# Issuing every DMA of a spectral mixer's forward and backward pass on SyncE's queue

## The chip, the cores and the metric

The kernel runs on one core of a Trainium2 chip. Its time is the device time of one execution in microseconds; several runs are made and the median is given. The five engines of the core are named as in the profile: PE (TensorE), DVE (VectorE), ACT (ScalarE), POOL (GpSimd) and SP (SyncE). A DMA is issued by an engine and carried out by the core's 16 DMA engines. In this kernel SP and ACT issue through a hardware queue each (q1 and q10 in the profile), POOL through a software queue (q0). DMA transposes are issued on SP alone.

## The reference

One pre-LayerNorm block with two mixers, x of 2048 x 448 in bfloat16, and all its gradients:

```python
def _A_ref(x, w_r, w_i):                      # spectral mixer
    X = rfft2(x.astype(float32), axes=(-2, -1))        # 2048 x 225 complex
    return irfft2(X * (w_r + 1j * w_i), s=(S, D)).astype(bfloat16)

def _B_ref(x, w1, b1, w2, b2):                # token MLP, F = 1792
    u = gelu(einsum("bsd,sf->bdf", layernorm(x), w1) + b1)
    return (einsum("bdf,fs->bds", u, w2) + b2).transpose(0, 2, 1)

h  = x + _A_ref(layernorm(x), w_r, w_i)
h2 = h + _B_ref(layernorm(h), w1, b1, w2, b2)
# outputs: h2, then the gradients of x, w_r, w_i, w1, b1, w2, b2 for grad_out
```

## The kernel before

The Fourier transforms are matrix products with tables of sines that the kernel makes itself: POOL writes counters (iota) and masks, DVE reduces the arguments, ACT takes the sines. A row transform (d_stage) is followed by a two-step column transform (s1_stage, s2_stage), and the inverse by s2_inv and inv_rows. Between the steps the rows are regrouped by small SP copies through SBUF: D2 (r_72 in the profile, written at L459) and D3 (r_73, written at L506).

In order of time, with the names that the prediction uses:

1. **Front.** x (xn, four loads on ACT, L193) and grad_out (go_tp, four loads on POOL, L194) come in. `load_w2T` (L187) brings rows of w2 in transposed on SP, into three buffers. The gradient of the hidden layer, dg = w2T x go (L567), is the filler: a generator that `fill(n)` advances by n matmuls between the steps of the spectral part. `fold_prep` (L433 to L437) folds pairs of LayerNorm rows into one of three buffers rF on DVE, and SP transposes them into rT. The spectral weights w_r and w_i are loaded by `w_io` (L398 and L400), 18 DMAs of 16 partitions each in rows of 225 elements, on POOL, into rG.
2. **Forward spectral stage.** s2_stage multiplies by the weights; the spectrum is kept in HBM (xspec_d, L615).
3. **Hidden layer (U stage).** `load_w1c` (L624) brings 256 columns of w1 at a time, two buffers, on POOL. The result of gelu and its derivative are made on ACT and DVE.
4. **Y stage.** `load_w2c` (L666) does the same for w2, into two buffers; L732 multiplies, `y_tail` (L737 to L740) loads the row of h from h_d on SP, adds on DVE and stores out_0 on POOL. Meanwhile SP transposes grad_out into goT (L719, L721) and the bias gradient (L714), which POOL stores (L715).
5. **dh stage.** SP transposes w1 (L789), L809 multiplies, `ln_bwd` (L777 to L783) is the LayerNorm backward, and the row transform of the spectral backward begins.
6. **Backward spectral stage.** SP transposes du (L818); POOL clears the pad columns (L819) and loads w_r and w_i again with `w_io`, into rD. Filler now are the gradients of w2 (L865, `gw2_gen`) and of w1 (L880, `gw1_gen`): `stream` (L851) transposes their left operands on SP into three buffers rst, the results go through ACT or DVE (L868, L883) into three buffers rO, and POOL stores them (L870, L885). The gradients of w_r and w_i are stored by `w_io` on POOL (L398).
7. **Tail.** For every one of 16 row blocks inv_rows ends in `gx_consumer`: an x load on SP (L901), ln_bwd, and the store of the gradient of x on SP (L905). Its buffers come from a ring of eight, five per step, so that DVE's tmp of a step (L781) takes the buffer from which the step before stores.

PE's order is written out by hand. The order on the other engines, SP's queue included, comes from a scheduler that goes by program order and its own estimate of when each instruction is ready. An instruction waits in its queue until its semaphores are there, and the next one behind it waits too.

Of the kernel before, what the change touches and what calls it, by code (L numbers as in the profile page):

```python
# [16 lines left out]
P = 128  # L17
S = 2048
D = 448
DF = 225  # L20
KW = 226
F = 1792
NFB = 14
# [36 lines left out]
def kernel(  # L60
# [138 lines left out]
    gp_.dma_start(out=gtail[:, 0:DC], in_=grad_out[0][S - 16:S, 3 * DC:D])  # L199

# [421 lines left out]
    def load_w1c(jp):  # L622
        w = w1c_ring.next()
        gp_.dma_start(out=w, in_=B_w1.rearrange("(p t) f -> p t f", t=NT)[:, :, 256 * jp:256 * jp + 256])  # L624
        return w
# [29 lines left out]
    gp_.dma_start(out=smr[0:NFB, 0, :], in_=B_b1.rearrange("(j p) -> j p", p=P))  # L655
    gp_.dma_start(out=smr[:, 1, :], in_=B_b2.rearrange("(j p) -> j p", p=P))
    for i, dst in ((0, b1col), (1, b2col)):
# [6 lines left out]
    def load_w2c(i):  # L664
        w2cs[i] = w2c_ring.next()
        gp_.dma_start(out=w2cs[i], in_=B_w2.rearrange("(j p) s -> p j s", p=P)[:, :, 256 * i:256 * i + 256])  # L666

# [46 lines left out]
    nc.sync.dma_start_transpose(out=gb1r[:], in_=gb1b[:])  # L714
    gp_.dma_start(out=out_5.rearrange("(j p) -> j p", p=P), in_=gb1r[0:NFB, :])  # L715

# [37 lines left out]
    for t in range(3, NT):  # L754
        py = ps_mm()
        y_head(t, 0, NFB, py)
        y_tail(t, py)
        gb2_part(t)
        if t == NT - 1:
            for q in range(3):  # L760
                gb2_part(q)
            ve.tensor_copy(out=gb2b[:], in_=gb2[:])
            gp_.dma_start(out=out_7.rearrange("(p t) -> p t", t=NT), in_=gb2b[:])
        if t % 2 == 1 and t // 2 + 2 < NT // 2:
            load_w2c(t // 2 + 2)
# [53 lines left out]
    gp_.memset(W_view_B[:, :, :, DF:KW], 0.0)  # L819
    w_io(W_view_B, A_w_r, A_w_i, False, gp_)  # L820
    srow = mem.tile([P, KW], BF16, name="srow")
# [37 lines left out]
    def gw2_gen():  # L859
        for j, gt in stream(NFB, rE):  # L860
            o = ost.next()
            for c in range(4):
                pw = ps_mm()
                for k in range(4):
                    nc.tensor.matmul(pw[:], lhsT=gt[0:DC, k, :], rhs=goT[0:DC, k, c * 512:(c + 1) * 512],  # L865
                                     start=(k == 0), stop=(k == 3))
                    if k == 3:
                        evac(out=o[:, c * 512:(c + 1) * 512], in_=pw[:])  # L868
                        if c == 3:
                            gp_.dma_start(out=out_6[j * P:(j + 1) * P, :], in_=o)  # L870
                    yield

    def gw1_gen():
        for t, ht in stream(NT, rB):
            o = ost.next()
            for c in range(4):
                n = 4 if c < 3 else 2
                pw = ps_mm()
                for k in range(4):
                    nc.tensor.matmul(pw[:, 0:n * P], lhsT=ht[0:DC, k, :], rhs=du_t[0:DC, 4 * c:4 * c + n, k, :],  # L880
                                     start=(k == 0), stop=(k == 3))
                    if k == 3:
                        evac(out=o[:, c * 512:c * 512 + n * P], in_=pw[:, 0:n * P])  # L883
                        if c == 3:
                            gp_.dma_start(out=o4[:, t, :], in_=o[:, 0:F])  # L885
                    yield
# [9 lines left out]
    s2_stage(bwd_mult, N_FILL_B[3], N_FILL_B[4])  # L896
    w_io(W_view_B, out_2, out_3, True, gp_)

# [40 lines left out]
```

## Time and profile before

| | |
|---|---|
| median of 3 runs | 554.54 us (553.81 to 555.45) |
| the profiled execution, its own time | 558.94 us |
| its span, first to last instruction | 556.8 us |
| mean granted PE clock | 0.876 |
| busy: PE, DVE, ACT, POOL | 386.8, 259.5, 232.8, 119.1 us |
| DMA bytes by queue: q1 (SP), q0 (POOL), q10 (ACT) | 43.41, 42.26, 1.84 MB |

The profile is one execution. Its slices are fortieths of the span, each digit a busy share in tenths. A line of the timeline has start and duration in us, the engine, the line of the kernel, the operation with output and input, and in brackets how long the engine had been idle and what ended that. "SPq" is SP's queue of issues; neighbouring instructions of one line are merged into one row, with their count and the time from the first start to the last end. In a line of the DMA queues stand packets, MB and the share of the time of 16 engines that the packets took; these shares add up to more than 1 where packets of two queues overlap. In the view by stretches each line has the stretch, its length, busy time and number of instructions of PE, PE's weight loads, DVE, ACT and POOL, then the granted clock, the DMA share (the sum of the queues) and GB/s.

### The profile page before, as it was taken

What the parts mean: (1) busy time and instruction counts of PE and PEld (TensorE: products, weight loads), DVE (VectorE), ACT (ScalarE), POOL (GpSimd) and SP (SyncE); (2) the same over time, 40 slices, a digit from 0 to 9 for tenths busy, and PEclk for the clock granted to TensorE, in tenths of its full rate; (3) what the DMA queues carried; (4) which work ended last, traced back from release to release, by engine and by line L of the source; (5) the groups of instructions that cost most, each with busy time, mean ns of one, the idle gap of its engine ahead of it and who ended that gap; (6) DMA issues with size and microseconds to landing.
All of it is one profiled execution on the core that took longest, in us unless ns stands there. A gap on an engine that the chain in (4) does not pass through costs nothing.

```text
span 556.8 us, 6068 instructions
## 1 busy us (share of the span) xinstructions
PE 386.8 (69%) x1920; PEld 192.2 (35%) x1920; DVE 259.5 (47%) x710; ACT 232.8 (42%) x477; POOL 119.1 (21%) x177
## 2 busy tenths in 40 slices
PE   0135287485739888986779999935449998399990
PEld 0012154141325444442334455512114443145540
DVE  6643176364207857770122877500005674035655
ACT  2131076173416554420122244723206877158882
POOL 8232059700100011030331000023111102411110
PEclk9967599796879999997798999977758999879995
DMA  9999979759956665259963999799995798986552
GB/s 121 216 97 111 131 137 171 118 141 178 214 131 144 221 202 161 77 129 142 233 187 115 175 191 201 149 217 77 69 102 198 188 208 165 141 224 193 182 175 83
DMA packets 137344, 87.89 MB, mean 158 GB/s; under 512 B 111136, under 2 KB 127584, under 8 KB 137184
## 3 DMA queue, kind: packets, MB, share of 16 engines
q1 hardware_dynamic: 125248, 43.41, 48.2%
q0 software_dynamic: 11488, 42.26, 33.4%
q10 hardware_dynamic: 576, 1.84, 1.4%
q8 instruction: 15, 0.25, 0.2%
q14 instruction: 17, 0.14, 0.1%
HBM read 29.40 MB, written 23.89 MB: 96 GB/s over the span
## 4 chain that ended last, share of the span: by engine, by line
DMA 41%; PE 21%; issue 14%; DVE 10%; POOL 7%; ACT 4%; SPq 2%; DVEq 0%; POOLq 0%; ACTq 0%
PE ps_mm L809 6%; PE ps_mm L732 5%; DMA rS<-in_B_w_dram 5%; DMA out_dram<-r_81 4%; DMA rG<-in_A_w_r_dram 4%; DMA r_72<-in_B_w_dram 4%; DMA rD<-in_A_w_i_dram 4%; DMA r_73<-r_78 3%; DMA rE<-in_B_w_dram 3%; DMA rC<-rD 3%; PE ps_mm L880 3%; PE ps_mm L865 2%; DMA xspec_d<-rS 2%; DMA rD<-in_A_w_r_dram 2%; DMA out_dram<-rO 2%
## 5 line engine op out<-in xcount | busy, mean ns | idle before, releaser
L567 PE MATMUL ps_mm<-rC,rE 128*128 128x448 bf16 x224 | 62.9, 418 | 50.0 <-DMA rE<-in_B_w_dram 50.0
L865 PE MATMUL ps_mm<-rG,rst 112*128 112x512 bf16 x224 | 59.7, 418 | 23.4 <-DMA rst<-rE 12.9
L732 PE MATMUL ps_mm<-rE,rS 128*128 128x448 bf16 x224 | 51.0, 396 | 15.5 <-DMA rS<-in_B_w_dram 15.5
L880 PE MATMUL ps_mm<-rC,rst 112*128 112x512 bf16 (+1 forms) x256 | 54.9, 363 | 3.3 <-ACT rO L883 2.0
L567 PEld LDWEIGHTS <-rE 128*128 128x128 bf16 x224 | 24.5, 113 | 78.5 <-DMA rE<-in_B_w_dram 51.6
L687 PE MATMUL ps_mm<-rB,r_72 128*128 128x448 bf16 x224 | 43.5, 353 | 6.6 <-DMA r_72<-in_B_w_dram 4.4
L809 PE MATMUL ps_mm<-rD,r_73 128*128 128x448 bf16 x224 | 43.5, 353 | 0.6 <-DMA r_73<-in_B_w_dram 0.6
L868 ACT CAST rO<-ps_mm 128x512 bf16<-128x512 f32 x54 | 30.4, 598 | 29.7 <-DMA out_dram<-rO 20.5
L865 PEld LDWEIGHTS <-rst 112*128 112x128 bf16 x224 | 23.6, 106 | 55.0 <-issue 20.9
L732 PEld LDWEIGHTS <-rS 128*128 128x128 bf16 x224 | 23.8, 108 | 42.5 <-DMA rS<-in_B_w_dram 17.2
L880 PEld LDWEIGHTS <-rst 112*128 112x128 bf16 x256 | 24.8, 100 | 26.2 <-issue 4.1
L883 ACT CAST rO<-ps_mm 128x512 bf16<-128x512 f32 (+1 forms) x61 | 30.4, 562 | 3.7 <-PE ps_mm L880 1.8
L528 PE MATMUL ps_ff<-csI,rAT 113*128 113x448 bf16 x128 | 31.2, 369 | 0.8 <-ACT rAT L517 0.5
L687 PEld LDWEIGHTS <-r_72 128*128 128x128 bf16 x224 | 21.6, 98 | 28.3 <-DMA r_72<-in_B_w_dram 5.9
L517 ACT CAST rAT<-ps_ff 113x512 bf16<-113x512 f32 x32 | 18.6, 589 | 30.2 <-PE ps_ff L514 30.2
L739 DVE SCALAR_TENSOR_TENSOR r_81<-ps_mm,b2col,r_81 128x448 bf16<-128x448 f32 x16 | 10.6, 681 | 43.9 <-DMA r_81<-h_d 37.3
L744 ACT ACTIVATE r_81<-rC 128x448 bf16<-128x448 bf16 x16 | 9.2, 576 | 51.9 <-DVE r_81 L739 38.9
L450 ACT CAST r_78<-ps_ff 128x452 bf16<-128x452 f32 x32 | 17.1, 539 | 30.7 <-PE ps_ff L447 30.5
L870 POOL DMA_DIRECT2D out_dram<-rO x14 | 7.5, 537 | 103.2 <-ACT rO L868 91.0
L809 PEld LDWEIGHTS <-r_73 128*128 128x128 bf16 x224 | 21.7, 97 | 22.9 <-issue 1.8
L514 PE MATMUL ps_ff<-RTm,r_73 128*113 128x128 bf16 x128 | 13.4, 235 | 18.5 <-DMA r_73<-r_78 18.2
L463 DVE TENSOR_SCALAR r_72<-r_72 128x904 bf16<-128x904 bf16 x8 | 2.7, 391 | 48.5 <-DMA r_72<-r_78 48.5
(211 smaller groups left out, 684.7 us busy)
## 6 DMA issues: line engine op xcount, KB each, us to landing
r_72<-in_B_w_dram POOLq DMA_DIRECT2D x7, 1024.0 KB, 7.1
rS<-in_B_w_dram POOLq DMA_DIRECT2D x8, 896.0 KB, 7.7
out_dram<-rO POOLq DMA_DIRECT2D x14, 512.0 KB, 5.6
out_dram<-rO POOLq DMA_DIRECT2D x16, 448.0 KB, 3.1
r_72<-r_78 SPq DMA_DIRECT2D x32, 113.0 KB
r_73<-r_78 SPq DMA_DIRECT2D x32, 113.0 KB
xspec_d<-rS SPq DMA_DIRECT2D x8, 226.0 KB
rS<-xspec_d SPq DMA_DIRECT2D x8, 226.0 KB
```

Source lines behind the costliest of these rows:

```text
L450: sc.copy(out=ab, in_=pv)
L514: nc.tensor.matmul(pa[0:KC, i * P:(i + 1) * P], lhsT=D3[:, s1, c_, KC * ch:KC * ch + KC], rhs=RTm[:], start=True, stop=True)
L517: sc.copy(out=aT[0:KC].rearrange("p a b -> p (a b)"), in_=pa[0:KC, :])
L528: nc.tensor.matmul(py[:, 0:D], lhsT=aT[0:KC, i, :], rhs=csI[0:KC, i // 2, i % 2, :], start=(i == 0), stop=(i == 3))
L567: nc.tensor.matmul(pg[:, 0:D], lhsT=wT[:, t, :], rhs=go_tp[:, t, :], start=(t == 0), stop=(t == NT - 1))
L687: nc.tensor.matmul(pu[:, 0:D], lhsT=w1c[:, t, jj * P:(jj + 1) * P], rhs=hln[:, t, :, :], start=(t == 0), stop=(t == NT - 1))
L732: nc.tensor.matmul(py[:, 0:D], lhsT=w2cs[t // 2][:, j, (t % 2) * P:(t % 2 + 1) * P], rhs=g_[:, j, :, :], start=(j == 0), stop=(j == NFB - 1))
L809: nc.tensor.matmul(pdh[:, 0:D], lhsT=wT[:, j, :], rhs=du[:, j, :, :], start=(j == 0), stop=(j == NFB - 1))
L865: nc.tensor.matmul(pw[:], lhsT=gt[0:DC, k, :], rhs=goT[0:DC, k, c * 512:(c + 1) * 512], start=(k == 0), stop=(k == 3))
L868: evac(out=o[:, c * 512:(c + 1) * 512], in_=pw[:])
L880: nc.tensor.matmul(pw[:, 0:n * P], lhsT=ht[0:DC, k, :], rhs=du_t[0:DC, 4 * c:4 * c + n, k, :], start=(k == 0), stop=(k == 3))
L883: evac(out=o[:, c * 512:c * 512 + n * P], in_=pw[:, 0:n * P])
```

## The change

Every DMA that ACT or POOL issued is issued by SP instead, on its hardware queue, in program order with the transposes: the loads of x and grad_out, the spectral weights' loads and stores, the biases, the chunks of w1 and w2, h_d's store, and the stores of out_0 and of the gradients of w1, w2 and the biases. POOL keeps its memsets, iotas and masks. Nothing else is changed; sizes, buffers and program order stay.

```diff
     for q in range(4):
-        nc.scalar.dma_start(out=xn[:, 4 * q:4 * q + 4, :], in_=x_pt[:, 4 * q:4 * q + 4, :])
-        gp_.dma_start(out=go_tp[:, 4 * q:4 * q + 4, :], in_=go_tp_d[:, 4 * q:4 * q + 4, :])
+        nc.sync.dma_start(out=xn[:, 4 * q:4 * q + 4, :], in_=x_pt[:, 4 * q:4 * q + 4, :])
+        nc.sync.dma_start(out=go_tp[:, 4 * q:4 * q + 4, :], in_=go_tp_d[:, 4 * q:4 * q + 4, :])
         if q < 2:
             w2Ts.append(load_w2T(q))
...
-    w_io(W_view_F, A_w_r, A_w_i, False, gp_)
+    w_io(W_view_F, A_w_r, A_w_i, False, nc.sync)
...
     def load_w1c(jp):
         w = w1c_ring.next()
-        gp_.dma_start(out=w, in_=...)
+        nc.sync.dma_start(out=w, in_=...)
...
-    gp_.dma_start(out=h_d.rearrange("(p t) d -> p t d", t=NT), in_=hn)
+    nc.sync.dma_start(out=h_d.rearrange("(p t) d -> p t d", t=NT), in_=hn)
...
     def load_w2c(i):
         w2cs[i] = w2c_ring.next()
-        gp_.dma_start(out=w2cs[i], in_=...)
+        nc.sync.dma_start(out=w2cs[i], in_=...)
...
     for q in range(2):
-        gp_.dma_start(out=go_pt[:, 8 * q:8 * q + 8, :], in_=go_pt_d[:, 8 * q:8 * q + 8, :])
+        nc.sync.dma_start(out=go_pt[:, 8 * q:8 * q + 8, :], in_=go_pt_d[:, 8 * q:8 * q + 8, :])
...
-        gp_.dma_start(out=out_0[0, t * P:(t + 1) * P, :], in_=h2)
+        nc.sync.dma_start(out=out_0[0, t * P:(t + 1) * P, :], in_=h2)
...
-    w_io(W_view_B, A_w_r, A_w_i, False, gp_)
+    w_io(W_view_B, A_w_r, A_w_i, False, nc.sync)
...
-                            gp_.dma_start(out=out_6[j * P:(j + 1) * P, :], in_=o)
+                            nc.sync.dma_start(out=out_6[j * P:(j + 1) * P, :], in_=o)
...
-                            gp_.dma_start(out=o4[:, t, :], in_=o[:, 0:F])
+                            nc.sync.dma_start(out=o4[:, t, :], in_=o[:, 0:F])
...
-    w_io(W_view_B, out_2, out_3, True, gp_)
+    w_io(W_view_B, out_2, out_3, True, nc.sync)
```

The same is done to the 16-row tail of grad_out (gtail), to the two bias loads, and to the stores of out_5 and out_7.

More of the change, by code (lines that the diff above doesn't have):

```diff
@@ L198 @@
     gp_.memset(gtail[:], 0.0)
-    gp_.dma_start(out=gtail[:, 0:DC], in_=grad_out[0][S - 16:S, 3 * DC:D])
+    nc.sync.dma_start(out=gtail[:, 0:DC], in_=grad_out[0][S - 16:S, 3 * DC:D])
     s448, s128, s2048 = _sin_scale(448), _sin_scale(128), _sin_scale(2048)
@@ L623, in load_w1c @@
         w = w1c_ring.next()
[L624 removed]
+        nc.sync.dma_start(out=w, in_=B_w1.rearrange("(p t) f -> p t f", t=NT)[:, :, 256 * jp:256 * jp + 256])
         return w
@@ L714 @@
     nc.sync.dma_start_transpose(out=gb1r[:], in_=gb1b[:])
-    gp_.dma_start(out=out_5.rearrange("(j p) -> j p", p=P), in_=gb1r[0:NFB, :])
+    nc.sync.dma_start(out=out_5.rearrange("(j p) -> j p", p=P), in_=gb1r[0:NFB, :])
     for c in range(3):
@@ L762 @@
             ve.tensor_copy(out=gb2b[:], in_=gb2[:])
-            gp_.dma_start(out=out_7.rearrange("(p t) -> p t", t=NT), in_=gb2b[:])
+            nc.sync.dma_start(out=out_7.rearrange("(p t) -> p t", t=NT), in_=gb2b[:])
         if t % 2 == 1 and t // 2 + 2 < NT // 2:
```

6 lines of the change are left out of this document (3 added, 3 removed).

## The prediction

> **What bounds the kernel now.** I read the page first: the totals, the slices, the queues and the chain that ended last.
>
> ```profile
> span 556.8 us, 6068 instructions
> PE 386.8 (69%) x1920; PEld 192.2 (35%) x1920; DVE 259.5 (47%) x710; ACT 232.8 (42%) x477; POOL 119.1 (21%) x177
> PE   0135287485739888986779999935449998399990
> DMA  9999979759956665259963999799995798986552
> q1 hardware_dynamic: 125248, 43.41, 48.2%
> q0 software_dynamic: 11488, 42.26, 33.4%
> DMA 41%; PE 21%; issue 14%; DVE 10%; POOL 7%; ACT 4%; SPq 2%; DVEq 0%; POOLq 0%; ACTq 0%
> ```
>
> TensorE is the busiest engine, but DMA is the largest share of the chain. Where the PE row is low (slices 0 to 4, and 26 to 29), the DMA row stands at 9: there the kernel waits for transfers. Half of the bytes already go through q1, the SyncE ring with all the transposes; the change brings q0's 42.26 MB into it (and ScalarE's 1.84 MB), so how the two rings behave together now is the question. The view by stretches answers it; its last three columns are granted clock, DMA share and GB/s. Under it are the queue lines (packets, MB, share) of the 66 to 110 and of the 380 to 404 us stretch.
>
> ```profile
> 40.00:66.00 26.00, 9.91 (x33) 3.83 (x32) 5.47 (x26) 2.66 (x4) 3.62 (x7) 0.63 1.24 104
> 66.00:110.00 44.00, 30.82 (x170) 17.22 (x169) 24.29 (x58) 20.85 (x43) 30.91 (x28) 0.89 0.88 153
> 303.00:357.00 54.00, 52.21 (x294) 28.30 (x293) 40.52 (x119) 22.32 (x61) 1.08 (x2) 1.00 0.91 172
> 380.00:404.00 24.00, 9.78 (x33) 3.65 (x31) 1.31 (x4) 5.62 (x10) 4.74 (x9) 0.74 1.28 72
> ...
> q1 hardware_dynamic: 21538, 6.69, 87.5%
> ...
> q0 software_dynamic: 490, 1.09, 72.0%
> q1 hardware_dynamic: 1298, 0.64, 55.6%
> ```
>
> With q1 nearly alone the engines move 153 to 172 GB/s. Where the w_r and w_i loads of w_io run beside it (40 to 66, 380 to 404) the shares add up to over 1 and the rate falls to 104 and 72 GB/s. A packet of q1 takes 16 x 44 us x 0.875 / 21538 = 28.6 ns in the first case and 16 x 24 x 0.556 / 1298 = 164 ns in the last. So these loads, 4096 rows of 450 bytes each time, are what is expensive, and they make everything beside them slow. One such row costs 16 x 24 x 0.72 / (1.09 MB / 450) = 114 ns of a DMA engine; divided by the overlap of 1.28 it is 89 ns.
>
> **Front (0 to 70 us).** The transfers issued at the start are x and go (1.84 MB each), three w2T transposes (2048 packets of 256 bytes each), w_io's 18 loads; then the fold transposes rT and the next w2T.
>
> ```profile
> 0.75 37.80 SPq L187 DMA_TRANSPOSE rE<-in_B_w_dram  x3
> 47.66 16.41 SPq L187 DMA_TRANSPOSE rE<-in_B_w_dram  x2
> 50.51 0.40 DVE L433 TENSOR_TENSOR rF<-rB 128x448 bf16<-128x448 bf16 x1 [15.46 <-DMA rT<-rF]
> 65.64 0.93 PE L567 MATMUL ps_mm<-rC,rE 128*128 128x448 bf16 x2 [10.98 <-DMA rE<-in_B_w_dram]
> 68.48 0.40 DVE L433 TENSOR_TENSOR rF<-rB 128x448 bf16<-128x448 bf16 x1 [12.50 <-DMA rT<-rF]
> ```
>
> ScalarE's queue, with the x loads alone, had this in the first 20 us:
>
> ```profile
> q10 hardware_dynamic: 460, 1.48, 34.9%
> ```
>
> SyncE is held 37.8 us by three transposes, so rT is late, VectorE waits for it twice, and the constants that POOL makes from VectorE's results come late in turn. In one ring this goes one after another. x and go: 1.48 MB took 16 x 20 x 0.349 = 112 us of engine time, 7.0 us on 16; 3.67 MB is 17 us. Three w2T at 128 packets per engine x 28.6 ns: 3.7 us each, 11 us. Then w_io: 256 rows per engine. Its price in the hardware ring is not in the trace. Ends: 28.6 ns per row (q1's packets alone) = 7.3 us, and 114 ns = 29 us. I take 89 ns, 23 us, since that row is the same transfer. I put w_io ahead of rT, the worse case, because it is ready once POOL has cleared rG, before the folds are. So w_io ends at 17 + 11 + 23 = 51 us; two rT (1024 packets each, 1.8 us) 55; w2T 3 at 58.5, against 65.64 now; w2T 4 and rT 2 at 64, against 68.48. Front: **-5 us** (ends -20 at 7.3 us, +1 at 29 us). POOL loses its DMA waits here; worth nothing by itself, since its first iota after them feeds a VectorE that waits for rT anyhow; without that cover it would add a gain.
>
> **Middle (110 to 237 us).** Two w1c loads (1 MB) and two w2c loads (0.9 MB) enter the ring among the reshapes of the spectrum. In the software queue they share with them, in the ring they stand before or behind them: D3's last rows wait for them wholly or not at all. I take 0; the ends are -8 and +8, as the wait for D3 now is:
>
> ```profile
> 163.53 1.08 PE L514 MATMUL ps_ff<-RTm,r_73 128*113 128x128 bf16 x8 [8.73 <-DMA r_73<-r_78]
> ```
>
> POOL's issue of such a load is 1.08 us and SyncE's issue of a copy 0.33 us (L666 and L905 below): 0.75 us saved per load, hidden where the load is a pair ahead. The wait of go's second load, h_d's store and the biases on SyncE block nothing that is due: the queue has only prefetches there.
>
> **Y stage (237 to 303 us).** w2c is double buffered, and TensorE waits for it four times.
>
> ```profile
> 245.21 1.08 POOL L666 DMA_DIRECT2D rS<-in_B_w_dram  x1 [19.81 <-PE ps_mm L732]
> 253.56 2.91 SPq L714 DMA_TRANSPOSE gb1r<-gb1b  x1
> 252.35 8.39 PE L732 MATMUL ps_mm<-rE,rS 128*128 128x448 bf16 x28 [4.41 <-DMA rS<-in_B_w_dram]
> 265.43 6.98 PE L732 MATMUL ps_mm<-rE,rS 128*128 128x448 bf16 x28 [4.70 <-DMA rS<-in_B_w_dram]
> 267.26 0.53 POOL L715 DMA_DIRECT2D out_dram<-gb1r  x1 [17.13 <-DMA gb1r<-gb1b]
> 274.81 12.45 PE L732 MATMUL ps_mm<-rE,rS 128*128 128x448 bf16 x56 [2.40 <-DMA rS<-in_B_w_dram]
> 291.24 12.45 PE L732 MATMUL ps_mm<-rE,rS 128*128 128x448 bf16 x56 [3.98 <-DMA rS<-in_B_w_dram]
> ```
>
> The waits are 15.5 us. w2c(2), issued at 245.21 now, would stand behind the goT transposes that hold SyncE to 253.56: about 8 us later, so the first wait grows to some 12 us; but then w2c(3) is there and the 4.70 goes, and w2c(4) is no longer behind the out_5 store, which held POOL 17.13 us, so 2.40 and a part of 3.98 go too. 8 - 4.7 - 2.4 - 3.98 = **-3 us** (ends +8 and -11). Behind w2c stand the h_d loads of the next tiles and the out_0 stores, which VectorE's additions wait for; four PSUM banks cover one pair.
>
> **Backward w_io (357 to 420 us).**
>
> ```profile
> 373.27 4.52 POOL L400 DMA_DIRECT2D rD<-in_A_w_r_dram  x8 [0.36 <-POOL rD L819]
> 400.92 1.31 DVE L463 TENSOR_SCALAR r_72<-r_72 128x904 bf16<-128x904 bf16 x4 [42.32 <-DMA r_72<-r_78]
> 406.90 0.57 POOL L870 DMA_DIRECT2D out_dram<-rO  x1 [1.04 <-DMA rD<-in_A_w_i_dram]
> 409.54 6.46 PE L865 MATMUL ps_mm<-rG,rst 112*128 112x512 bf16 x16 [12.91 <-DMA rst<-rE]
> ```
>
> POOL issues w_io from 373.27 on, the third gw2 store stands behind it until 406.90, and TensorE waits for the transposes rst until 409.54. On SyncE the 18 loads wait for the du_t transpose and POOL's memset just the same, with rT, the r_72 reshapes and rst behind them. From 373.27, 23 us: 396; five reshapes and two rst, about 6 us: 402, against 409.54. **-7 us** (ends -23 and -1, by the two ends of the row price).
>
> **Tail (490 to 550 us).** Each step is closed by its own gx store: VectorE's next L781 waits for it (rows of the timeline, of the chain, and of the list of issues).
>
> ```profile
> 530.07 0.40 DVE L781 TENSOR_SCALAR r_81<-r_81,lcol 128x448 bf16<-128x448 bf16 x1 [0.73 <-DMA out_dram<-r_81]
> 528.28 1.69 DMA out_dram<-r_81
> 530.17 0.54 POOL L885 DMA_DIRECT2D out_dram<-rO  x1 [3.86 <-ACT rO L883]
> 531.64 0.33 SPq L905 DMA_DIRECT2D out_dram<-r_81  x1
> 531.64 3.72 DMA out_dram<-r_81
> out_dram<-rO POOLq DMA_DIRECT2D x16, 448.0 KB, 3.1
> ```
>
> The store takes 1.69 us alone and 3.72 us when a gw1 store was issued 1.5 us before it. In one ring it waits for such a store wholly. Some 14 steps; I take a third of them hit by 1 us: **+5 us** (ends 0 and 14 x 2.03 = +28).
>
> **Sum.** -5 + 0 - 3 - 7 + 5 = -10 us. The profiled execution took 558.94 us (556.8 us span and 2.1 around it), which gives 549; the median of the runs is 554.54, 4.4 lower, and the forecast stands against it: **544 us**.
>
> **A rule against this.** The Trainium skill, "DMA: Bandwidth & Descriptors", section "Issuing engines are not separate DMA queues", says that DMAs of all issuers run on the same 16 engines and interleave, so that the choice of issuer saves sequencer time alone. By that the change would be a wash but for the issue (rival C). The trace agrees in part: shares add to 1.28, but the rate falls to 72 GB/s, so it does matter what interleaves with what.
>
> **Rivals.**
> A: rows of 450 bytes cost more in the ring, where nothing interleaves with them. Place: the front and 373 us. From 29 us per w_io the gains there are gone; at 164 ns per row (what q1's packets took beside them) it is 42 us: front +14, w_io backward +12, tail +5, Y -3: 583 us. For it: no such row was ever in q1. Against it: 89 ns already holds sharing.
> B: SyncE's order in the tail. A gw1 store that waits for ScalarE's cast stands ahead of the gx store each step: +28 instead of +5, 567 us. It decides from 15 us on, 1.1 us per step. For it: 3.72 against 1.69. Against: the other step quoted closes in 1.69 us beside the same gw1 stores.
> C: a wash: what the front gains is given back because POOL's constants and TensorE's fill set the start of the spectral stage:
>
> ```profile
> 77.19 7.33 POOL L300 TENSOR_SCALAR Ut<-rO,cols 128x512 bf16<-128x512 bf16 x4 [5.56 <-ACT rO L298]
> ```
>
> -10 becomes 0, 554 us.
>
> **Chances.** Forecast 0.46, of which its own range is 514 (w_io at 7.3 us: -20 -3 -23 +5) to 557 (at 29 us: +1 -3 -1 +5); A 0.18, B 0.22, C 0.14. The measurement tells 0.3%, 1.7 us, from no change. C splits 0.04 faster, 0.07 same, 0.03 slower; of the forecast, 0.01 is same. So 0.49 faster, 0.08 same, 0.43 slower. The range leaves out the forecast's lowest end, a tenth, and most of what lies at and beyond A, another: 521 to 580.
>
> **What would show it.** In the trace after: no q0, and in 0 to 60 us a rate well over 104 GB/s; the first rT landing near 53 us and TensorE's second stage at 58; w_io's rows near 89 ns; TensorE back at gw2 near 402 us; the first w2c wait longer and the later ones gone; the gx store at 1.7 us in two thirds of the steps. Wrong it would be if the transposes stay as slow beside w_io in one ring, or if the queue line of SyncE shows long waits for ScalarE or VectorE with loads behind them that TensorE lacks.

## The result, and the profile after

With every DMA on SyncE the kernel takes **501.69 us** (median of 4 runs, 501.09 to 502.19) against 554.17 us for the kernel before in the same comparison: a ratio of 0.906, 95% interval 0.902 to 0.910. I had forecast 544 us, in 521 to 580. The direction was right; the gain is five times what I had. The medians of the kernel before lie between 547.4 and 554.2 us in the comparisons of this text, so ratios are used, each against the runs of before on the same chip. An execution over 1.5% above the fastest of its kernel counts as slow; the ratios are of the others alone, the medians of all, and the profiles of before, of the two kernels with four chunks and of the one with go alone are of slow executions.

The page of the changed kernel: span, engines, PE's slices, the only queue of weight, and the chain that ended last.

```profile
span 500.2 us, 6019 instructions
PE 376.9 (75%) x1920; PEld 189.9 (38%) x1920; DVE 261.1 (52%) x709; ACT 235.1 (47%) x478; POOL 39.5 (8%) x50
PE   2553865967798999639789999750899996969960
q1 hardware_dynamic: 177320, 87.50, 81.9%
PE 40%; DMA 32%; DVE 17%; ACT 5%; SPq 4%; issue 3%; DVEq 0%; POOLq 0%; POOL 0%; ACTq 0%
```

q0 is gone. PE's busy time fell by 9.9 us (386.8 to 376.9, at a mean granted clock of 0.876 and 0.901), so some 47 of the 56.6 us of span are waiting that is gone (PE's first slices read 25538 for 01352); TensorE is now the largest share of the chain, ahead of DMA. PE runs its instructions in the same order in both kernels, so stages can be set side by side. The table has the time from the first instruction of one stage to that of the next (PE's own, but SyncE's issue for L818), from the profiled executions (558.94 us before, above its median; 502.19 after):

| stretch | before | after | difference | forecast |
|---|---|---|---|---|
| start to the row transform (L444) | 66.4 | 46.4 | -20.0 | -5 |
| L444 to the column transform (L475) | 40.9 | 39.5 | -1.4 | |
| L475 to the inverse (L514) | 56.2 | 41.7 | -14.5 | 0 |
| L514 to the hidden layer (L687) | 23.7 | 22.4 | -1.3 | 0 |
| U: L687 to L732 | 50.0 | 47.8 | -2.2 | 0 |
| Y: L732 to L809 | 66.3 | 62.4 | -3.9 | -3 |
| dh: L809 to du's transpose (L818) | 54.3 | 55.0 | +0.7 | |
| L818 to the backward L475 | 62.1 | 50.9 | -11.2 | -7 |
| backward L475 to backward L514 | 68.3 | 58.4 | -9.9 | 0 |
| backward L514 to the end | 68.6 | 75.7 | +7.1 | +5 |

Four stretches hold the gain. The view by stretches (start to end, length, busy time of PE, its weight loads, DVE, ACT, POOL, granted clock, DMA share, GB/s), first of before, then of after:

```profile
0.00:14.00 14.00, 0.00 (x0) 0.00 (x0) 9.73 (x38) 2.86 (x3) 11.49 (x25) 1.00 1.02 120
357.00:420.00 63.00, 31.14 (x117) 13.15 (x116) 4.13 (x11) 16.88 (x32) 13.32 (x25) 0.72 1.14 131
```

```profile
0.00:14.00 14.00, 3.32 (x8) 1.12 (x9) 12.87 (x52) 0.46 (x1) 7.73 (x19) 1.00 0.90 228
315.00:365.00 50.00, 27.34 (x111) 12.04 (x110) 2.30 (x8) 17.19 (x33) 0.25 (x1) 0.73 1.12 158
326.00:344.00 18.00, 6.79 (x23) 3.09 (x23) 0.00 (x0) 4.14 (x8) 0.25 (x1) 0.59 1.25 121
```

The DMA engines are about as busy as before and move more: 228 GB/s for 120 in the first 14 us, 158 for 131 in the backward stretch. (Of the kernels below, the six with x and go on the queues of before move 120 to 201 GB/s in these 14 us, the ten with both on SyncE 223 to 241.) SyncE's queue in the changed kernel (start, time, line, operation; "x9" is nine in a row) shows the new order. The time is how long the issue held SyncE, which for a transpose is not the time to its landing (the rst transpose issued at 435.59 holds SyncE 1.52 us and lands 5.90 us after that start):

```profile
1.66 4.19 SPq L187 DMA_TRANSPOSE rE<-in_B_w_dram  x1
6.99 4.05 SPq L187 DMA_TRANSPOSE rE<-in_B_w_dram  x1
14.28 7.63 SPq L400 DMA_DIRECT2D rG<-in_A_w_r_dram  x9
22.68 2.32 SPq L400 DMA_DIRECT2D rG<-in_A_w_i_dram  x3
25.83 4.05 SPq L187 DMA_TRANSPOSE rE<-in_B_w_dram  x1
29.98 4.03 SPq L437 DMA_TRANSPOSE rT<-rF  x3
34.06 3.04 SPq L400 DMA_DIRECT2D rG<-in_A_w_i_dram  x6
119.56 2.71 SPq L506 DMA_DIRECT2D r_73<-r_78  x4
122.32 0.61 SPq L624 DMA_DIRECT2D r_72<-in_B_w_dram  x1
123.04 6.38 SPq L666 DMA_DIRECT2D rS<-in_B_w_dram  x2
326.48 4.70 SPq L400 DMA_DIRECT2D rD<-in_A_w_r_dram  x9
332.25 9.55 SPq L400 DMA_DIRECT2D rD<-in_A_w_i_dram  x9
426.13 8.35 SPq L398 DMA_DIRECT2D out_dram<-rD  x11
```

And PE's timeline at the places where it waits (in brackets the idle time before and what ended it), first one line of before, then the changed kernel:

```profile
25.35 5.28 PE L567 MATMUL ps_mm<-rC,rE 128*128 128x448 bf16 x16 [25.35 <-DMA rE<-in_B_w_dram]
```

```profile
7.88 1.67 PE L567 MATMUL ps_mm<-rC,rE 128*128 128x448 bf16 x4 [7.88 <-DMA rE<-in_B_w_dram]
45.70 0.93 PE L567 MATMUL ps_mm<-rC,rE 128*128 128x448 bf16 x2 [8.62 <-DMA rE<-in_B_w_dram]
127.58 0.67 PE L514 MATMUL ps_ff<-RTm,r_73 128*113 128x128 bf16 x8 [3.71 <-DMA r_73<-r_78]
351.33 5.30 PE L865 MATMUL ps_mm<-rG,rst 112*128 112x512 bf16 x12 [17.20 <-DMA rst<-rE]
424.49 1.07 PE L514 MATMUL ps_ff<-RTm,r_73 128*113 128x128 bf16 x8 [1.83 <-DMA r_73<-r_78]
441.54 3.13 PE L880 MATMUL ps_mm<-rC,rst 112*128 112x512 bf16 x8 [4.20 <-DMA rst<-rB]
```

These answer to the lines of before: the first matmul of the front starts at 7.88 us (25.35 before), the second stage at 45.70 (65.64), the wait for D3 is 3.71 (8.73). The last row, a 4.20 us wait for rst behind eleven w_io stores, is the new one.

### The profile page after: what moved, and what is told of

Same layout as the page of the kernel before. It is cut to its first block, busy times and chain, and to the rows that moved or that the text cites. A ratio compares the mean times of both kernels' runs of the same rounds, so it can differ in the third digit from the quotient of the medians.

```text
span 500.2 us, 6019 instructions
## 1 busy us (share of the span) xinstructions
PE 376.9 (75%) x1920; PEld 189.9 (38%) x1920; DVE 261.1 (52%) x709; ACT 235.1 (47%) x478; POOL 39.5 (8%) x50
## 4 chain that ended last, share of the span: by engine, by line
PE 40%; DMA 32%; DVE 17%; ACT 5%; SPq 4%; issue 3%; DVEq 0%; POOLq 0%; POOL 0%; ACTq 0%
DMA out_dram<-r_81 9%; PE ps_mm L865 8%; PE ps_mm L687 7%; PE ps_mm L809 5%; PE ps_mm L567 5%; PE ps_mm L880 4%; DVE stats L547 3%; PE ps_mm L732 3%; DMA r_73<-r_78 3%; DMA r_73<-in_B_w_dram 2%; DMA rC<-rD 2%; DMA rD<-in_A_w_i_dram 2%; DMA rE<-in_B_w_dram 2%; DMA xspec_d<-rS 2%; DVE r_81 L783 2%
## 5 line engine op out<-in xcount | busy, mean ns | idle before, releaser
L865 PE MATMUL ps_mm<-rG,rst 112*128 112x512 bf16 x224 | 56.2, 400 | 17.9 <-DMA rst<-rE 17.2
L732 PE MATMUL ps_mm<-rE,rS 128*128 128x448 bf16 x224 | 44.9, 361 | 17.7 <-DMA rS<-in_B_w_dram 17.7
L687 PE MATMUL ps_mm<-rB,r_72 128*128 128x448 bf16 x224 | 45.0, 362 | 2.9 <-DVE rB L646 1.9
L809 PE MATMUL ps_mm<-rD,r_73 128*128 128x448 bf16 x224 | 43.7, 352 | 1.5 <-DMA r_73<-in_B_w_dram 1.5
L868 ACT CAST rO<-ps_mm 128x512 bf16<-128x512 f32 x56 | 31.7, 596 | 26.8 <-PE ps_mm L865 26.5
L732 PEld LDWEIGHTS <-rS 128*128 128x128 bf16 x224 | 21.9, 100 | 40.5 <-DMA rS<-in_B_w_dram 19.9
L744 ACT ACTIVATE r_81<-rC 128x448 bf16<-128x448 bf16 x16 | 9.2, 576 | 48.8 <-DVE r_81 L739 38.1
L687 PEld LDWEIGHTS <-r_72 128*128 128x128 bf16 x224 | 22.2, 100 | 25.5 <-issue 5.0
L809 PEld LDWEIGHTS <-r_73 128*128 128x128 bf16 x224 | 21.6, 98 | 24.0 <-DMA r_73<-in_B_w_dram 2.6
L450 ACT CAST r_78<-ps_ff 128x452 bf16<-128x452 f32 x32 | 17.2, 541 | 22.5 <-PE ps_ff L447 22.4
L517 ACT CAST rAT<-ps_ff 113x512 bf16<-113x512 f32 x32 | 18.4, 584 | 14.1 <-PE ps_ff L514 14.0
L477 ACT CAST rS<-ps_ff 128x452 bf16<-128x452 f32 x30 | 16.2, 542 | 15.2 <-PE ps_ff L476 10.6
L777 ACT ACTIVATE r_81<-ps_mm 128x448 bf16<-128x448 f32 x16 | 8.7, 543 | 29.8 <-PE ps_mm L809 28.7
```

The source lines that it names most:

```text
L450: sc.copy(out=ab, in_=pv)
L477: evac(out=xc[:, i, :, :], in_=pv)
L517: sc.copy(out=aT[0:KC].rearrange("p a b -> p (a b)"), in_=pa[0:KC, :])
L687: nc.tensor.matmul(pu[:, 0:D], lhsT=w1c[:, t, jj * P:(jj + 1) * P], rhs=hln[:, t, :, :], start=(t == 0), stop=(t == NT - 1))
L732: nc.tensor.matmul(py[:, 0:D], lhsT=w2cs[t // 2][:, j, (t % 2) * P:(t % 2 + 1) * P], rhs=g_[:, j, :, :], start=(j == 0), stop=(j == NFB - 1))
L809: nc.tensor.matmul(pdh[:, 0:D], lhsT=wT[:, j, :], rhs=du[:, j, :, :], start=(j == 0), stop=(j == NFB - 1))
```

## The experiments

Two theories stood against each other for most runs. **Theory:** a DMA transpose and copies of another ring make each other slow, whatever the copies are; one ring puts them one after another. **Rival:** what costs is a particular transfer or POOL's software queue, and any other queue would do. In the recorded expectations they are theory 1 and, for the software queue, theory 2. The edits are small, most of them which engine issues what.

**1. w_io alone, both ways.**

```diff
 (kernel before; second run: forward only, nc.scalar)
-    w_io(W_view_F, A_w_r, A_w_i, False, gp_)
+    w_io(W_view_F, A_w_r, A_w_i, False, nc.sync)
-    w_io(W_view_B, A_w_r, A_w_i, False, gp_)
+    w_io(W_view_B, A_w_r, A_w_i, False, nc.sync)
 (third run: changed kernel, these two lines back to gp_)
 (fourth run: changed kernel, only the stores back)
-    w_io(W_view_B, out_2, out_3, True, nc.sync)
+    w_io(W_view_B, out_2, out_3, True, gp_)
```

> The kernel before, with only the 36 weight loads of w_io (forward and backward) on SyncE. Theory 1 (the rows of 450 bytes were slow and made the transposes slow because two rings shared the DMA engines): the front shortens most of the 20 us that the whole change gave, the first row transform on TensorE (L444) starts by 52 us (66.4 before, 46.4 after), and the backward wait shortens by about 10 us: some 525 us. Rival (the front's gain is x, grad_out and the order of the other engines): L444 stays at 60 us or later and the time within 8 us of 554.

Measured: 533.02 us, ratio 0.978 (0.968 to 0.989). L444 starts at 63.4 us, as the rival had it: four of the kernels here have the front of before, and L444 at 61.5 to 66.4 us, so no gain in the front is shown. The stretch after L818 goes from 62.1 to 54.5 us, less than in any kernel with these loads on POOL (55.8 to 62.1). SyncE's queue and PE's first matmul of this kernel:

```profile
0.75 24.96 SPq L187 DMA_TRANSPOSE rE<-in_B_w_dram  x2
```

```profile
28.94 7.84 PE L567 MATMUL ps_mm<-rC,rE 128*128 128x448 bf16 x32 [28.94 <-DMA rE<-in_B_w_dram]
```

Without w_io beside them, the two w2T transposes still hold SyncE 25 us, beside x and go alone.

> The kernel before, with only the 18 forward weight loads on ScalarE's hardware queue: a hardware queue, but another ring than the transposes. If what cost was the software queue (theory 2), the front shortens as with SyncE, L444 by 52 us, about 540 us. If what cost was that two rings share the DMA engines (theory 1), L444 stays at 60 us or later, 550 to 556 us.

Measured: 539.98 us, 0.987 (0.980 to 0.993). L444 at 56.4 us, 10 earlier than before and 10 later than in the changed kernel, and between the two expectations. Why ScalarE's ring does better here than SyncE's (63.4) is open.

> The changed kernel, with only the 36 weight loads back on GpSimd. Theories 1 and 2: most of the front's 20 us and of the 11 us up to the backward spectral stage are lost again: 525 to 532 us. Rival (the rest of the change carries the gain): 502 to 510 us.

Measured: 517.99 us, 0.944 (0.935 to 0.954) where the changed kernel has 0.906, between the two expectations. L444 is back at 55.6 us, the stretch after L818 at 55.8. The third w2T, 4.05 us in the changed kernel, meets w_io's loads, and so does the fourth, behind which three rT stand here:

```profile
14.30 19.02 SPq L187 DMA_TRANSPOSE rE<-in_B_w_dram  x1
37.04 10.93 SPq L187 DMA_TRANSPOSE rE<-in_B_w_dram  x1
48.07 4.51 SPq L437 DMA_TRANSPOSE rT<-rF  x3
```

> The changed kernel, with only the 18 stores of the weight gradients back on GpSimd. In the changed kernel TensorE waits 5.9 us at 435.6 us for a transpose that stands behind eleven of these stores in SyncE's queue. If that is what makes the last stage 7 us longer (75.7 against 68.6 us), the time falls to about 496 us. Rival: the stores on the other ring take their share of the engines from D3's last rows, as before (9.7 us wait at 478 us), and the time rises by 3 to 8 us.

Measured: 503.51 us, 0.919 (0.911 to 0.926), with the time moved: backward L475 to L514 takes 65.9 us instead of 58.4, the tail 70.3 instead of 75.7. On SyncE's queue and on PE:

```profile
415.83 6.27 SPq L851 DMA_TRANSPOSE rst<-rB  x1
434.21 1.20 SPq L851 DMA_TRANSPOSE rst<-rB  x1
```

```profile
430.54 1.07 PE L514 MATMUL ps_ff<-RTm,r 128*113 128x128 bf16 x8 [12.15 <-DMA r<-r]
```

A transpose of the same size holds SyncE 6.27 us while the stores of the other ring run (POOL issues them until 425.5) and 1.20 later; PE waits for D3 too, 12.15 us instead of 1.83. The tail gains what the first expectation said, and D3 loses it again, as the rival said.

**2. x and go at the start.**

```diff
 (kernel before; go_sp has the second line alone, xgo_act has nc.scalar in it)
-        nc.scalar.dma_start(out=xn[:, 4 * q:4 * q + 4, :], in_=...)
-        gp_.dma_start(out=go_tp[:, 4 * q:4 * q + 4, :], in_=...)
+        nc.sync.dma_start(out=xn[:, 4 * q:4 * q + 4, :], in_=...)
+        nc.sync.dma_start(out=go_tp[:, 4 * q:4 * q + 4, :], in_=...)
```

> The kernel before, with only the eight loads of x and grad_out at the start on SyncE, in one ring with the transposes of w2. In the changed kernel the first two transposes held SyncE for 4.2 and 4.1 us, and in both kernels with x and grad_out on other queues for 1.4 and 23.4 us, with 228 GB/s in the first 14 us against 120 to 125. Theory 1 (copies in other rings beside transposes slow both): two transposes are issued by 12 us again, L444 starts at 52 to 58 us (66.4 before), some 10 us off the total. Rival (the w_io loads, still on GpSimd, take back what is won): L444 at 63 us or later, less than 4 us off.

Measured: 534.45 us, 0.972 (0.962 to 0.981). L444 at 47.9 us: 18.5 of the front's 20 us from these eight loads alone (13.6 against the earliest of the four fronts that are as before).

```profile
0.00:14.00 14.00, 3.33 (x8) 1.14 (x9) 12.85 (x50) 0.00 (x0) 11.58 (x26) 1.00 0.93 225
```

225 GB/s in the first 14 us, as with everything on SyncE (228), for 120 in the kernel before. w_io is still on POOL here, as in the run with L444 at 55.6; but here two rT are issued at 31.04, ahead of the fourth w2T, and there at 48.07, behind it. So what w_io's ring is worth seems to hang on the order that the scheduler finds, by several us.

> The kernel before, with the loads of grad_out on ScalarE's hardware queue, behind those of x: no software queue is in use in the first 10 us, but two rings are. If the software queue is what slows the transposes (theory 2), the second transpose is issued within 6 us and L444 comes at 52 to 58 us. If two rings are enough (theory 1), the second issue still takes 15 us or more, the rate in the first 14 us stays under 170 GB/s, and L444 stays at 62 us or later.

Measured: 537.60 us, 0.976 (0.960 to 0.993); L444 at 52.1 us, and 194 GB/s in the first 14 us. The front is as the rival expected it, not the theory (62 us or later); the rate decides nothing, since kernels with the front of before have up to 201: transposes and copies overlap here too, but x and go are on ScalarE's ring alone, and 14.3 us of the front are gained. PE's first matmul waits for a load of go and no longer for w2T:

```profile
10.85 1.65 PE L567 MATMUL ps_mm<-rC,rE 128*128 128x448 bf16 x4 [10.85 <-DMA rC<-in_grad_out_dram]
```

The second w2T holds SyncE 12.31 us here, for 23.41 before and 4.05 in the changed kernel: the overlap still costs, but less.

> The kernel before, with only the four loads of grad_out at the start on SyncE; x stays on ScalarE's ring. The first L444 was at 47.9 us with x and grad_out on SyncE, at 52.1 with both on ScalarE, at 66.4 before. If the software queue beside the transposes makes up the difference, L444 comes at 47 to 53 us. If any second ring does, x's loads keep it at 56 us or later.

Measured: 545.37 us, 0.988 (0.982 to 0.994); L444 at 66.3 us, nothing gained in the front, as the theory expected. x on ScalarE's ring is enough to slow the second w2T; the third, beside w_io on POOL, holds SyncE 20.45 us:

```profile
8.08 15.47 SPq L187 DMA_TRANSPOSE rE<-in_B_w_dram  x1
```

But the run above uses the same three queues and has a front 14.2 us shorter; SyncE issues its first rT at 44.13 us there and at 56.71 here. So neither the software queue nor "any second ring" explains all these fronts. How much of that is the order of SyncE's queue, no run here separates.

**3. Is it the rings, or the overlap in time?** Up to here "one ring" and "not at the same time" could not be told apart. This run keeps x and go on their own rings and lets the transposes begin when they have landed: ScalarE writes one element of each into the transposes' buffers first, which the transposes then overwrite.

```diff
 (kernel with w_io's loads on SyncE, of experiment 1)
     for q in range(4):
         nc.scalar.dma_start(out=xn[...], in_=...)
         gp_.dma_start(out=go_tp[...], in_=...)
-        if q < 2:
-            w2Ts.append(load_w2T(q))
+    for v in w2T_ring.views:
+        sc.copy(out=v[:, 0, 0:1], in_=go_tp[:, NT - 1, 0:1])
+        sc.copy(out=v[:, 0, 1:2], in_=xn[:, NT - 1, 0:1])
+    for q in range(2):
+        w2Ts.append(load_w2T(q))
```

> Based on the kernel with only w_io's loads on SyncE (x on ScalarE's queue, go on POOL's): ScalarE writes one element of go's and of x's last tile into each of the three w2T buffers, so that the first three w2T transposes start only when x and go have landed. Theory (it is the overlap in time of DMA transposes with copies of another ring that costs): although x and go stay on other rings, each of these transposes now holds SyncE 3 to 6 us instead of 12 to 25, and the first L444 starts between 48 and 57 us, against 63.4 without the wait and 46.4 with everything on SyncE; time 517 to 528. Rival (copies in rings of their own are slow, or are slow to begin, whatever lies beside them): x and go land no earlier, the wait is added to the front, L444 starts at 62 us or later, and the time is 533 or more.

Measured: 522.08 us, 0.946 (0.940 to 0.952). L444 (L447 in this file) starts at 48.8 us, 14.6 earlier than without the wait, though the transposes begin 14 us later. Its stretch, its queues in 0 to 14 us, SyncE's queue and PE:

```profile
0.00:14.00 14.00, 0.00 (x0) 0.00 (x0) 9.48 (x35) 2.14 (x6) 11.70 (x25) 1.00 0.92 283
```

```profile
q10 hardware_dynamic: 576, 1.84, 37.6%
q0 software_dynamic: 512, 1.84, 34.8%
```

```profile
14.49 8.46 SPq L187 DMA_TRANSPOSE rE<-in_B_w_dram  x2
```

```profile
23.86 7.93 PE L570 MATMUL ps_mm<-rC,rE 128*128 128x448 bf16 x32 [23.86 <-DMA rE<-in_B_w_dram]
```

x and go, on two other rings, one of them the software queue, are both there in 14 us at 283 GB/s; two transposes then hold SyncE 8.46 us, not 25. From its issue to PE's first matmul the first w2T takes 9.4 us (14.49 to 23.86), for 28.2 without the wait (0.75 to 28.94) and 6.2 in the changed kernel (1.66 to 7.88). So at the start it is the overlap in time that costs: with x and go in the same queues as before, both the copies and w2T are quicker once they do not overlap. How much an overlap costs does depend on the queues, as experiment 2 shows. The order of SyncE's queue is not the same in the two kernels either (three rT go out from 23.05 us here, while the second is issued at 32.33 there), so the 14.6 us of L444 need not all be the overlap's. The one ring is a way to forbid the overlap.

**4. The chunks of w1 and w2 in the spectral stage.**

```diff
 (kernel before; both loads, all chunks -- or, in the chunks4 runs, the first two of each,
  on nc.scalar or nc.sync; after_chunks_pool is the changed kernel with both back on gp_)
-        gp_.dma_start(out=w, in_=B_w1...)
+        nc.sync.dma_start(out=w, in_=B_w1...)
-        gp_.dma_start(out=w2cs[i], in_=B_w2...)
+        nc.sync.dma_start(out=w2cs[i], in_=B_w2...)
```

> The kernel before, with only the chunk loads of w1 and w2 on SyncE. By the same theory the stretch from L475 to L514 falls from 56 to 45 us or less, and the time by 8 to 15 us. Rival: the chunks wait on SyncE for TensorE with the reshapes of the spectrum behind them, the stretch stays at 53 us or more and the time within 4 us of the kernel before.

Measured: 531.62 us, 0.969 (0.960 to 0.978). L475 to L514 takes 44.8 us and Y 58.6.

> The kernel before, with the same four chunk loads on SyncE, the later chunks left on GpSimd. Both theories: the stretch from L475 to L514 falls to 43 to 48 us. The Y stage (L732 to L809, 66.3 us before, 58.6 with all chunks on SyncE) stays within 2 us of before, if its gain comes from the later chunks.

Measured: 543.89 us, 0.979 (0.964 to 0.993). L475 to L514 is 45.6 us: the first four chunks do it. Y stays (67.8).

> The kernel before, with only the first two chunks of w1 and the first two of w2 on ScalarE's hardware queue, in a ring of their own. They are the four loads that lie beside the reshapes of the spectrum (L475 to L514, 56.2 us before, 41.7 after, 44.8 with all chunks on SyncE). If the gain there comes from the chunks standing in order in the reshapes' own ring, this stretch stays at 51 us or more. If the software queue is what slowed the reshapes, it falls to 47 us or less here too.

Measured: 547.88 us, 0.997 (0.992 to 1.002), no difference; L475 to L514 is 55.2 us. The same four loads on another hardware ring bring nothing.

> The changed kernel, with only the chunk loads of w1 and w2 (w1c, w2c) back on GpSimd. The stretch from the first column matmul (L475) to the inverse rows (L514) is 41.7 us after and 56.2 before. If its 14.5 us come from the reshapes of the spectrum no longer sharing the DMA engines with these chunks, 10 us or more of them are lost: 511 to 520 us. Rival (they come from the front, or from TensorE's fill standing ready): less than 4 us lost.

Measured: 520.77 us, 0.947 (0.938 to 0.957): 51.2 us from L475 to L514, so 9.5 of the 14.5 us are lost again, and 69.6 in Y. PE's wait for D3, first with four chunks on ScalarE, then in this last kernel:

```profile
160.11 1.10 PE L514 MATMUL ps_ff<-RTm,r 128*113 128x128 bf16 x8 [8.86 <-DMA r<-r]
```

```profile
134.25 1.08 PE L514 MATMUL ps_ff<-RTm,r 128*113 128x128 bf16 x8 [9.81 <-DMA r<-r]
```

Here it is the order in the ring: the changed kernel issues one w1c amid D3's copies, at 100.34, but D3's last four at 119.56 and the next w1c and two w2c behind them (122.32 and 123.04), and D3 is there 5.67 us after its last issue; on another ring, hardware or software, the megabytes of the prefetch are carried beside D3's copies. The stage also has w2T transposes, which hold SyncE 8.37 and 5.34 us in the kernel before and 3.81 and 3.68 in the changed one. They are not what makes the stage long: with the four chunks on ScalarE's ring they hold it 2.59 and 2.03 us, and the stage is 55.2 us.

**5. The tail.** First the w_io stores written behind inv_rows in program order, on SyncE; then in addition the gw1 stores on POOL.

```diff
 (changed kernel)
-    w_io(W_view_B, out_2, out_3, True, nc.sync)
 ... (inv_rows and its loop)
+    w_io(W_view_B, out_2, out_3, True, nc.sync)
 (second run, in addition)
-                            nc.sync.dma_start(out=o4[:, t, :], in_=o[:, 0:F])
+                            gp_.dma_start(out=o4[:, t, :], in_=o[:, 0:F])
```

> The changed kernel, with the 18 stores of the weight gradients moved behind the inverse rows in program order, still on SyncE, so that the transposes rst and the stores of gw1 go between them. With these stores on GpSimd the last stage fell from 75.7 to 70.3 us, but D3's last rows came 12.2 us late. Here D3 keeps its place: the spectral stage stays near 58 us, the last stage falls to 69 to 72 us, and the time to 496 to 499 us. Rival: the gx stores of the tail then wait behind them, and nothing is won, 501 to 505 us.

Measured: 496.60 us, 0.901 (0.893 to 0.909); the last stretch 70.7 us instead of 75.7, Y 65.0 instead of 62.4, the others within 1 us of the changed kernel.

> Everything on SyncE, with w_io's sums stored behind the inverse reshapes (the kernel of 496.6 us), and the 16 gw1 stores (L885) on POOL's queue. Theory (what is left of the tail's loss, 70.7 against 68.6 us, is the gx store waiting in the ring for a gw1 store, as the prediction had it): last stretch 68 to 69.5 us, 493 to 496 us. Rival (stores of another ring slow the rst transposes and the stores of gx, as copies of another ring did elsewhere): last stretch 71 us or more, 497 to 503.

Measured: 498.44 us, 0.903 (0.896 to 0.909); the last stretch 70.4 us. In the tail neither theory holds: the gw1 stores neither delay the gx stores nor gain by another ring. But the stretch before, in which gw1's stores begin, takes 60.6 us, where the other seven kernels with w_io's stores on SyncE have 57.1 to 58.4; that is the rival's effect, in one profile.

**6. Side by side on one chip**, the changed kernel, the one with late w_io stores, and the changed kernel with gw2's stores (L870) on POOL.

> The changed kernel itself once more, so that the kernel with late w_io stores can be set beside it on one chip. Expected: 0.900 to 0.910 of the kernel before, with a last stretch (from the backward L514 to the end) near 75.7 us in its trace.

> The changed kernel with the stores of w_io's sums (L398) written behind inv_rows. Theory (the eleven w_io stores ahead of the rst transposes are the tail's loss): last stretch 70 to 71.5 us against the changed kernel's 75 to 76, and 3 to 7 us faster than it on the same chip. Rival (what the stores give back in the trace is lost again elsewhere, or was the difference of two chips): within 2 us of it.

> The changed kernel with gw2's 14 stores (L870) on POOL's queue as before. The stretch from du's transpose to the backward L475 is 50.9 us in the changed kernel and 54.5 with w_io's loads alone on SyncE. Theory (stores of another ring slow the rst transposes and the reshapes beside them): 53 to 56 us here, 503 to 508 us in all. Rival (these 3.6 us come from elsewhere, w_r and w_i being earlier in the changed kernel): 50 to 52 us, and a total within 2 us of the changed kernel.

Measured: 499.91 us (0.911, 0.906 to 0.915), 495.99 (0.905, 0.901 to 0.910) and 503.41 (0.918, 0.910 to 0.925). The last stretch is 76.1 us in the first and 71.3 in the second, so the tail's loss is w_io's stores; the medians differ by 3.9 us. Single runs still overlap (496.2 to 502.3 against 495.1 to 500.1), so for the whole time this is likely, not certain. SyncE's queue in the second kernel:

```profile
424.96 2.94 SPq L398 DMA_DIRECT2D out_dram<-rD  x3
428.00 1.43 SPq L851 DMA_TRANSPOSE rst<-rB  x1
```

The stores now stand between the transposes, a few at a time, not eleven in front. With gw2's stores on POOL the stretch from L818 to the backward L475 is 52.4 us, 51.5 in the first kernel: between the two expectations, 1 of the 3.6 us in question. The kernel of experiment 3, which also has gw2's stores on POOL and w_io's loads on SyncE, has 51.3 there, so the 3.6 us are within the scatter of one profile. The median, 3.5 us above the first kernel's, is where the theory had it, but two runs at 507 us make it; the other four, 499.5 to 505.7, begin within the first kernel's 496.2 to 502.3. So no cost of these stores is shown.

**All runs together.** One execution of one kernel varies by some us in a stretch, so each cause was looked at over all 19 profiles (before, the changed kernel and the runs above), sorted by where the transfers of that stretch are issued; us, lowest to highest, with the number of profiles:

| stretch | transfers | on SyncE | on another queue |
|---|---|---|---|
| L475 to L514 | first chunks | 40.7 to 45.6 (10) | 50.0 to 56.2 (9) |
| Y | later w2c chunks | 58.6 to 65.0 (9) | 64.6 to 69.6 (10) |
| L818 to backward L475 | w_io loads | 49.9 to 54.5 (10) | 55.8 to 62.1 (9) |
| backward L475 to L514 | w_io stores | 57.1 to 60.6 (8) | 64.0 to 68.4 (11) |
| backward L514 to end | w_io stores ahead of inv_rows | 74.8 to 77.2 (5) | 67.6 to 71.3 (14) |

The 14 of the last row have these stores on POOL or, three of them, behind inv_rows. Four of the five rows do not overlap; Y's do, by 0.4 us.

The front divides too: L444 is at 44.2 to 47.0 us in the eight kernels with x, go and w_io's loads on SyncE, and at 61.5 to 66.4 in the four that have the front of before. So do the w2T transposes themselves. The second holds SyncE 3.8 to 4.7 us with x and go on SyncE (10 profiles), 2.2 behind them, 12.3 with both on ScalarE's ring, 15.5 with x alone there, and 23.4 to 26.9 with x there and go on POOL (6). The third holds it 3.0 to 7.1 us with w_io's loads on SyncE (10), 6.7 with them on ScalarE's ring, and 11.3 to 20.5 with them on POOL (8). A part of the rival stands, then: beside ScalarE's ring the transposes lost less than beside POOL's software queue.

## Why the prediction was wrong, step by step

**The reading of "shares over 1".** I took sums of 1.24 and 1.28 for two rings in each other's way, as my description of the view did, and priced a w_io row from them. The stretch 326 to 344 of the changed kernel has 1.25 with one ring: the sum does not tell rings apart. What does is the rate, or how long one and the same transpose takes.

**Front, -5 for -20: the size was off, by two terms and the order.** Right was the mechanism, transfers one after another, and w2T at 3.7 us (4.19 and 4.05). The first failed term is x and go, 7.0 us for 1.48 MB and so 17 us. The row that I used (460 packets at 34.9% of 20 us, 16 x 20 x 0.349 / 460 = 243 ns each) came from a stretch in which transposes ran beside. Where none do, x is 16 x 14 x 0.376 / 576 = 146 ns per packet (run of experiment 3), and with go 16 x 14 x (0.376 + 0.348) / 16 = 10.1 us. In the changed kernel x, go and two w2T are all issued by 13.5 us, where I had 24. The second is w_io, priced too high too: 18 loads are issued in 13.0 us of the queue (7.63, 2.32 and 3.04) and in 15.3 the second time (326.48 to 341.80), where I took 23. And I put w_io ahead of rT as the worse case: three rT went ahead of the last six loads, at 29.98, so rT was issued by 34 us where I had it at 55. I priced the one ring with durations paid in the mixed state that it ends. That is the error that matters; w_io's loads, which I called "what is expensive", bring the front no gain by themselves that is clear of the scatter, though putting them back on POOL costs the changed kernel 9.2 us there; x and go alone bring most of it. The prediction's front is also a sum of transfers alone. The chain of after runs through VectorE's work (tables and LayerNorm) from 1.1 to 32.1 us, then through SyncE's third rT and six w_io loads to the w2T that TensorE's second stage waits for:

```profile
37.20 8.46 DMA rE<-in_B_w_dram
```

So VectorE, which the sum leaves out, is what a still faster start of the ring would meet.

**Middle, 0 for -14.5: wrong.** The step that failed is "D3's last rows wait for them wholly or not at all. I take 0": they do not wait, because three of the four loads are issued behind D3's last rows. The ends of 8 were wrong too, since I looked at the last wait alone. The chain of before has two more in this stage, and the chain of after their successors (its last two rows belong to the tail, below):

```profile
123.72 9.09 DMA r_73<-r_78
135.62 8.88 DMA xspec_d<-rS
```

```profile
97.19 3.83 DMA xspec_d<-rS
105.18 4.61 DMA xspec_d<-rS
121.67 5.67 DMA r_73<-r_78
435.59 5.90 DMA rst<-rB
484.02 1.65 DMA out_dram<-r_81
```

9.09 + 8.88 and the wait of 8.73 at L514 are 26.7 us; 3.83 + 4.61 + 5.67 are 14.1. This is 12.6 of the 14.5, as a rough sum, since pieces of the chain are landings and not waits of PE. By PE's own time the stage has 21.7 us idle before and 10.4 after, and 34.6 and 31.4 busy (granted clock 0.80 and 0.90). The chunks' place alone divides all profiles (40.7 to 45.6 us, and 50.0 to 56.2).

**Y, -3 for -3.9: the number is luck.** The first wait grew to 12.00 us, as forecast, but the later ones did not go: they add 5.7 us, so that the waits for w2c grew. What fell is the time of the matmuls themselves, as the page has it for L732 (busy time, mean ns of one, then the wait), before and after:

```profile
L732 PE MATMUL ps_mm<-rE,rS 128*128 128x448 bf16 x224 | 51.0, 396 | 15.5 <-DMA rS<-in_B_w_dram 15.5
```

```profile
L732 PE MATMUL ps_mm<-rE,rS 128*128 128x448 bf16 x224 | 44.9, 361 | 17.7 <-DMA rS<-in_B_w_dram 17.7
```

The waits give +2.2 us and the matmuls -6.1, at a granted clock of 0.92 in this stretch for 0.87 before. The prediction has no term for that. PE's busy time here is 44.8 to 47.9 us in the nine kernels with the later chunks on SyncE and 48.7 to 50.9 in the other ten; why the clock differs no run shows.

**Backward w_io, -7 for -11.2: the mechanism right, the size low.** PE waits for rst until 351.33, 36 us after L818 is issued (409.54 - 357.8 = 52 before). The kernels with w_io's loads alone on SyncE have 54.5 and 51.3 us here, so most of it is the term for w_io's rows, 23 us where the queue shows 15.3. The next stretch, where the prediction has no term, gave 9.9: w_io's stores ran beside rst and D3 on POOL's queue, and with them back there it is 65.9 us. That step was left out.

**Tail, +5 for +7.1: the size, by the wrong step.** The gx store that I had behind a gw1 store lands in 1.65 to 1.9 us, as at 484.02, in all but two of the 13 steps that the chain has (2.53 and 2.58), and taking the gw1 stores away changes 0.3 us. The loss is rst behind w_io's stores: PE waits 4.20 us and the chain has it as one piece, 5.90 at 435.59. The prediction has no line on what stands behind these 18 stores. The 2 us left are open: 70.4 to 71.3 us in the three kernels with late stores, 67.6 to 70.5 in those with these stores on POOL.

**The rivals.** A (dearer rows) fell: about 60 ns per row from the issues above (15.3 us for 256 rows per engine), not 89 or more. B's loss is there but small, and from another member of the queue. C, a wash, fell. The Trainium skill, "DMA: Bandwidth & Descriptors", section "Issuing engines are not separate DMA queues", says that the choice of issuer saves issue time alone; the runs do not agree, at 0.906, and most of it at places where DMA, not an issue, ended the wait. The same page's section "Queues, rings and completion order" says that a DMA engine takes packets from its queues in turns. That agrees with experiment 4, where the prefetch delays D3 from any other ring (55.2 us) and not from behind it in the same ring (45.6). It does not by itself give the front, where the rate is 120 to 201 GB/s in the kernels with x and go on other queues and 223 to 241 in those with both on SyncE.

## What to carry to other kernels

Keep DMA transposes and bulk copies apart in time: in one ring if that is simplest, or by a dependence that starts the one when the other has landed. Put a prefetch behind the small copies that the next step needs, in the same ring; then look for what bulk store has got in front of a transpose there, and write it later. When a change ends an overlap, price it with durations from stretches without that overlap, and if there are none, widen the range to the rate of the best stretch in the trace.

## What the runs showed of the hardware that I had not expected

The first w2T transpose, from its issue to the first matmul on it, takes 6.2 us in one ring with x and go, 9.4 us behind them on other rings, and 24.6 to 28.2 us beside x on ScalarE's ring and go on POOL's queue; beside x alone it takes 17.6 us, and with both on ScalarE's ring at most 10.1, since there a load of go ended the wait. The copies lose too: over the first 14 us x takes 146 ns per packet with no transpose beside it and 198 to 265 beside transposes (six kernels). In that time copies and transposes together moved 120 to 201 GB/s with x on ScalarE's ring and go on POOL's queue, 194 and 196 with none of the two on POOL's but at least one on ScalarE's, 223 to 241 with both in SyncE's ring, and 283 with the transposes held back. ScalarE's hardware queue was no better a place for the chunks than POOL's software queue (55.2 us for 56.2). Why a transpose and a copy hurt each other no run here shows; nor is it separated how much of the front hangs on the order that the scheduler gives DVE, ACT and SyncE, beyond the one place named in experiment 2.
